# Joining four partition groups of softmax maxima and sums by scalar copies instead of tensor transposes

## The chip, the cores and the metric

The kernel runs on one core of a Trainium2 chip. A core has engines that run side by side, each working through its own instruction queue in order: PE (TensorE) multiplies matrices, with PEld as its weight loads; DVE (VectorE), ACT (ScalarE) and POOL (GpSimd) work on tiles; SP (SyncE) issues most DMAs. SBUF is the on-chip memory with 128 partitions, PSUM the memory that PE writes its results to. The metric is device time in microseconds of one execution.

## The reference

```
xn = layernorm(x)                                   # x: 2048 x 640
q  = xn @ wq                                        # 32 heads of 128
k, v = the last 512 rows of each head's cache
s  = softmax(q k^T / sqrt(128)) v, all heads, @ wo  # 2048 x 640
g  = silu(relu(xn @ w1 + b1)^2 @ w2 + b2)           # 640 -> 1728 -> 640
out = x + s * g
```

All data are float32. The softmax runs over 512 keys, with the row maximum subtracted before the exponential.

## The kernel before

**Products.** Each float32 operand is split into a rounded part (`hi`) and a rest (`lo`), and a product is three matmuls: hi*hi, hi*lo, lo*hi (`triple`). ACT makes hi by a copy, DVE or POOL makes lo by a subtraction.

**Stages.** First comes the gate network for three of the four 512-row tiles, up to about 300 us. Then come the 128 attention units that fill most of the time: `units` runs over two halves of the rows, 16 pairs of heads, two row tiles of a half, and the two heads of a pair. One unit `i` is one head against 512 queries. The gate network of the last row tile is worked in after that, with parts of it in the first three units (`early_up`, `late_relu`, `late_square`, `early_split`).

**One unit.** Scores are held transposed, keys on partitions and queries in columns: 512 keys are 4 chunks of 128 partitions, in two PSUM tiles of two banks each, `s` (`s_mm`). A query's maximum and sum thus lie across partitions. They are found so:

- `max_fold` runs once for each of the two score tiles. It calls `fold`, a DVE reduction over a 128 x 1024 tile that transposes each 32 x 32 block on the way, so that each group of 32 partitions gives its own maximum of every query. The result `rdm` has 4 partition groups x 32 lines, and in its columns the 4 key chunks x 16 query blocks.
- `gather` (DVE) reduces the 4 chunks, giving `r1m` with 128 x 16 elements.
- `turn` (PE) transposes it into PSUM, `ptm`, 16 x 128, and so brings the four partition groups side by side.
- `row` (DVE) reduces the four groups into `rowm`, 16 x 32. Then SP stores these 512 numbers to DRAM (`m_d`) and loads them back, broadcast to all 128 partitions (`bm`).
- `shift` (DVE) subtracts `bm` from the two score tiles, which frees their banks for the next unit's `s_mm`; `expo` (ACT) takes the exponential; `p_hi` (ACT) and `p_lo` (POOL) split it into `pt`; `s_add` (POOL) adds the two halves to `su`.
- The sums go the same way, one period later: `s_fold` on `su` in SBUF (tile `rds`), `gather` (`r1s`), `turn` (`pts`), `row` (`rows`, with a reciprocal), DRAM (`s_d`), broadcast (`bs`).
- `v_mm` multiplies `pt` with the values into `o`; `o_norm` (DVE) scales `o` by `bs`; `o_hi` and `o_lo` split it into `ot`; `r_mm` (PE) and `r_acc` (DVE, tile `acc`) bring it through the output weights.

In between, `q_mm`, `q_hi` and `q_lo` make the queries of unit `i + 2`, and `load_raw` and `prep` load and split the next weights (on ACT the copies `wk`, `wq`, `wv`, `wo`, on POOL their rests).

**Order.** All of this is written into a list `plan` by `at(when, f, ...)` and issued sorted by `when`, in a nominal period of 12.4. The engines that are called through `Ordered` keep that order in their queues, whatever is ready. So an instruction that waits holds up all that is behind it on its engine. The instructions of the units carry line 72, that of the helper, in the profile, and are told apart by their tiles.

Of the kernel before, what the change touches and what calls it, by code (L numbers as in the profile page):

```python
# [8 lines left out]
F32 = mybir.dt.float32  # L9
F32R = mybir.dt.float32r  # L10
AF = mybir.ActivationFunctionType
ALU = mybir.AluOpType
AX = mybir.AxisListType

P = 128
NT = 512
# [4 lines left out]
def kernel(  # L21
# [21 lines left out]
    FC = (F + P - 1) // P  # L43
    KC = W // P
# [8 lines left out]
    dpool = ctx.enter_context(tc.tile_pool(name="dram", bufs=1, space=bass.MemoryType.DRAM))  # L53

    ident = cpool.tile([P, P], F32, name="ident")
# [8 lines left out]
    class Ordered:  # L64
# [13 lines left out]
    pe, dve, act, pool, sp = (  # L78
        Ordered(e) for e in (nc.tensor, nc.vector, nc.scalar, nc.gpsimd, nc.sync)
    )  # L80
# [18 lines left out]
    psx = ctx.enter_context(tc.tile_pool(name="psx", bufs=1, space=PSUM))  # L99

    FA = FC - 3
# [76 lines left out]
    def ln_rows(t, mv, xs):  # L178
        pm = psx.tile([P, NT], F32, tag="x", name=f"pmv{t}")
        nc.tensor.transpose(pm[: 2 * NB, :P], mv.rearrange("p a b -> p (a b)"), ident)  # L180
        row = xp.tile([2 * NB, P], F32, tag="lr", name=f"lr{t}", bufs=1)
        nc.vector.tensor_copy(row, pm[: 2 * NB, :P])
        d = dpool.tile([2, NT], F32, name=f"mv_d{t}")
        nc.sync.dma_start(d.rearrange("a (b p) -> (a b) p", p=P), row)
        bc = []
        for i in range(2):
            m = xp.tile([P, D], F32, tag="mr", name=f"mr{t}_{i}")[:, :NT]
            nc.sync.dma_start(m, d[i : i + 1, :].to_broadcast([P, NT]))
            bc.append(m)
        return bc, xs  # L190
# [136 lines left out]
    def mlp_step(n):  # L327
# [47 lines left out]
    PERIOD = 12.4  # L375
    B32 = 32
    AHEAD = 2
    NQ = NT // B32
# [4 lines left out]
    XT, ACC, KT, VV, WQ, WO, Q, E, SC, MB, RD, PT, PO, OT, RB, QPS, FX, CL, PRS, RAW = (  # L383
        {} for _ in range(20)
    )
# [81 lines left out]

    def fold(rd, k, src, op):
        dve.tensor_reduce(
            rd[:, k * NQ * 2 : (k + 1) * NQ * 2],  # L470
            src.rearrange("p c (b i) -> p (c b) i", i=B32),
            axis=AX.X,
            op=op,
            apply_transpose=True,
        )

    def max_fold(i, k):
        if k == 0:
            RD[i, "m"] = ap.tile([P, KC * NQ], F32, tag="rd", name=f"rdm{i}", bufs=3)
        fold(RD[i, "m"], k, SC[i, k], ALU.max)  # L480

    def gather(i, what):
        rd = RD.pop((i, what))
        n = rd.shape[1] // NQ
        r1 = ap.tile([P, NQ], F32, tag="r1", name=f"r1{what}{i}", bufs=4)
        dve.tensor_reduce(
            r1,
            rd.rearrange("p (c b) -> p b c", b=NQ),
            axis=AX.X,
            op=ALU.max if what == "m" else ALU.add,  # L490
        )
        RD[i, what] = r1

    def turn(i, what):
        pm = psx.tile([P, NT], F32, tag="x", name=f"pt{what}{i}")
        pe.transpose(pm[:NQ, :P], RD.pop((i, what)), ident)
        RD[i, what] = pm

    def row(i, what):
        pm = RD.pop((i, what))  # L500
        r = ap.tile([NQ, B32], F32, tag="row", name=f"row{what}{i}", bufs=4)
        dve.tensor_reduce(
            r,
            pm[:NQ, :P].rearrange("p (a i) -> p i a", i=B32),
            axis=AX.X,
            op=ALU.max if what == "m" else ALU.add,
        )
        if what == "s":
            dve.reciprocal(r, r)
        d = dpool.tile([NQ, B32], F32, tag=f"{what}_d", name=f"{what}_d{i}", bufs=4)  # L510
        sp.dma_start(d, r)
        bc = ap.tile([P, NT], F32, tag=f"b{what}", name=f"b{what}{i}", bufs=2)
        sp.dma_start(bc, d.rearrange("a b -> (a b)")[None, :].to_broadcast([P, NT]))
        (MB if what == "m" else RB)[i] = bc
# [25 lines left out]
        pool.tensor_tensor(RD[i, "su"], E[i, 0], E[i, 1], op=ALU.add)  # L540

    def s_fold(i):
        RD[i, "s"] = ap.tile([P, 2 * NQ], F32, tag="rd", name=f"rds{i}", bufs=3)
        fold(RD[i, "s"], 0, RD.pop((i, "su")), ALU.add)

    def v_mm(i, c):
        hf, g, t, h = units[i]
# [75 lines left out]
    LW, LH, LPH, LPY, LR = {}, {}, {}, {}, {}  # L623
# [98 lines left out]
        else:  # L722
            act.activation(r, ph, AF.Relu, bias=bias)

    def late_square(f):
        pool.tensor_tensor(LR[f], LR[f], LR[f], op=ALU.mult)

    def late_split(f):
        n = chunks[f][1]
# [83 lines left out]
    ap = ctx.enter_context(tc.tile_pool(name="at", bufs=2))  # L813
# [4 lines left out]
    def at(when, f, *a):  # L818
        plan.append((max(when, 0.0), len(plan), f, a))
# [16 lines left out]
    for t in range(TPH):  # L836
        for c in range(DC):
            k, late = divmod(c + 1 - t, 2)
# [17 lines left out]
    for i in range(NU):  # L856
        t0 = i * PERIOD

        def on(when, f, *a):
            at(t0 + when, f, *a)  # L860

        hf, g, t, h = units[i]
        for c in range(KC):
            on(0.68 * c, s_mm, i, c)
        if i + AHEAD < NU:
            q_at = 3.45 if i % G and i > UPG else 4.3
            for c in range(DC):
                on(q_at + 0.68 * c, q_mm, i + AHEAD, (c,))
            on(q_at + 3.5, q_hi, i + AHEAD)
            on(q_at + 4.1, q_lo, i + AHEAD)  # L870
        on(1.4, max_fold, i, 0)
        on(2.8, max_fold, i, 1)
        on(3.95, gather, i, "m")
        on(5.0, turn, i, "m")
        on(5.4, row, i, "m")
        on(10.4, shift, i, 0)
        on(11.6, shift, i, 1)
        on(11.7, expo, i, 0)
        on(12.7, p_hi, i, 0)
        on(13.8, expo, i, 1)  # L880
        on(14.8, p_hi, i, 1)
        on(13.9, p_lo, i, 0)
        on(16.2, s_add, i)
        on(PERIOD + 6.2, s_fold, i)
        on(PERIOD + 7.4, gather, i, "s")
        on(PERIOD + (8.45 if i < FC - FA - 1 else 9.2), turn, i, "s")
        on(PERIOD + 9.6, row, i, "s")
        on(18.6, p_lo, i, 1)
        for c in range(KC):
            on(PERIOD + 8.5 + 0.68 * c, v_mm, i, c)  # L890
        on(2 * PERIOD + 4.2, o_norm, i)
        on(2 * PERIOD + 4.9, o_hi, i)
        on(2 * PERIOD + 5.5, o_lo, i)
        if i % G == G - 1:
            for d in range(DC):
                last = i == NU - G - 1
                if i < NU - 1:
                    for when, js in (R_AT_END if last else R_AT)[d]:
                        on(when, r_mm, i, d, js, (R_BANK_END if last else R_BANK)[d])
                    on(when + 0.68 * len(js), r_acc, i, d)  # L900
                if g == NG - 1 and hf == 0:
                    w = (NU // 2 + 9 + 4 * (t * DC + d)) * PERIOD
                    for k, n in enumerate("sxg"):
                        at(w + k * PERIOD - 0.6, load_finish, n, 0, t, d)
                    at(w + 3 * PERIOD - 0.7, finish, 0, t, d)
# [10 lines left out]
    for item in order:  # L916
        kind, n = item[0], int(item[1:] or 0)
# [37 lines left out]
    for f, u in sorted(UP_AT.items()):  # L955
        at(LOAD.get(f, PREP.get(f - 2, 0) + 0.9), late_load, 1, f)
        when = PREP.setdefault(f, u - 5.0)
        at(when, late_prep, 1, f)
        for c in range(DC):
            at(u + 0.68 * c, late_up, f, UP_BANK[f] if f < len(UP_BANK) else (f + 1) % 2, c)  # L960
        relu, square, split = STEPS_AT.get(f, (u + 3.5, u + 4.3, u + 5.7))
        at(relu, late_relu, f, "kv"[f % 2])
        at(square, late_square, f)
        at(split, late_split, f)
# [8 lines left out]
    for k, f in enumerate(range(FA, FC)):  # L973
        t0 = k * PERIOD
        for c in range(DC):
            at(t0 + 8.0 + 0.1 * c, early_up, f, 0, c)
        at(t0 + 10.6, late_relu, f, "s")
        at(t0 + 12.0, late_square, f)
        at(t0 + PERIOD + 7.6, early_split, f)
    at(z + 2.0, late_x)  # L980
    for d in range(DC):
# [51 lines left out]
```

## Time and profile before

| | us |
|---|---|
| three runs, median (lowest to highest) | 2020.71 (2017.9 to 2021.19) |
| profiled execution, its own time | 2021.47 |
| its span, first to last instruction | 2019.7 |
| PE busy | 1987.9 (98%) |
| DVE busy | 1535.8 (76%) |
| POOL busy | 1375.4 (68%) |
| ACT busy | 985.8 (49%) |

The profile is one execution. Engine lines give busy time, share of the span and number of instructions. The chain of work that ended last is followed back from the last instruction, at each step to what released it; its shares say on what the end depended. A group line names the code line, engine, operation, the tile written and the tiles read, shapes and count, then busy time and the mean ns of one, then the idle time of the engine just before these instructions and what ended it. A wait line says who waited for whom, for how long in all, how many times, and the longest. A timeline line has the start, the time until the last of the merged instructions ended, the engine, and in brackets the idle time before. The granted clock of PE was 0.999 of full speed.

### The profile page before, as it was taken

What the parts mean: (1) busy time and instruction counts of PE and PEld (TensorE: products, weight loads), DVE (VectorE), ACT (ScalarE), POOL (GpSimd) and SP (SyncE); (2) the same over time, 40 slices, a digit from 0 to 9 for tenths busy, and PEclk for the clock granted to TensorE, in tenths of its full rate; (3) what the DMA queues carried; (4) which work ended last, traced back from release to release, by engine and by line L of the source; (5) the groups of instructions that cost most, each with busy time, mean ns of one, the idle gap of its engine ahead of it and who ended that gap; (6) DMA issues with size and microseconds to landing.
All of it is one profiled execution on the core that took longest, in us unless ns stands there. A gap on an engine that the chain in (4) does not pass through costs nothing.

```text
span 2019.7 us, 25025 instructions
## 1 busy us (share of the span) xinstructions
PE 1987.9 (98%) x8832; PEld 1609.3 (80%) x8832; DVE 1535.8 (76%) x2252; ACT 985.8 (49%) x1266; POOL 1375.4 (68%) x754
## 2 busy tenths in 40 slices
PE   7999999999999999999999999999999999999998
PEld 6788887788888888888887788787878888788877
DVE  5532337788888888888887778888888888888864
ACT  4432335555555555555554455555555555555533
POOL 1121227788777777777777788788888888877841
PEclk9999999999999999999999999999999999999999
DMA  4431454322333332333335433333333333333344
GB/s 140 128 113 29 177 196 132 99 90 89 90 89 89 90 89 90 90 91 90 91 96 159 154 95 105 110 110 111 110 110 111 110 112 110 96 91 90 106 146 140
DMA packets 126862, 220.32 MB, mean 109 GB/s; under 512 B 21542, under 2 KB 36304, under 8 KB 125456
## 3 DMA queue, kind: packets, MB, share of 16 engines
q1 hardware_dynamic: 123744, 204.28, 33.6%
q0 software_dynamic: 2992, 14.43, 1.8%
q8 instruction: 70, 1.15, 0.2%
q14 instruction: 56, 0.46, 0.1%
HBM read 194.26 MB, written 24.39 MB: 108 GB/s over the span
## 4 chain that ended last, share of the span: by engine, by line
PE 88%; DMA 6%; DVE 2%; POOL 1%; ACT 1%; issue 1%; SPq 0%; POOLq 0%; DVEq 0%
PE pq L72 20%; PE r L72 19%; PE s L72 17%; PE o L72 15%; DMA bm<-m_d 2%; PE py L96 2%; PE py L97 2%; PE py L95 2%; PE ph L96 2%; PE ph L95 2%; PE ph L97 2%; PE ly L72 2%; DMA m_d<-rowm 1%; PE lu L72 1%; DMA w1r<-in_w_dram 1%; DVE e L72 1%
## 5 line engine op out<-in xcount | busy, mean ns | idle before, releaser
L72 POOL TENSOR_TENSOR pt<-e,pt 128x1024 fp32r<-128x1024 f32 x256 | 617.5, 2412 | 296.1 <-ACT pt L72 296.1
L72 PE MATMUL r<-ot,wo 128*128 128x512 f32 x1920 | 496.9, 389 | 0.5 <-DVE acc L72 0.5
L72 PE MATMUL pq<-ax,wq 128*128 128x512 f32 x1920 | 473.1, 396 | 0.1
L72 ACT ACTIVATE e<-e 128x1024 f32<-128x1024 f32 x256 | 269.5, 1053 | 370.6 <-DVE e L72 331.6
L72 PEld LDWEIGHTS r<-ot,wo 128*128 128x128 f32 x1920 | 360.2, 188 | 75.9 <-DVE acc L72 0.9
L72 PEld LDWEIGHTS pq<-ax,wq 128*128 128x128 f32 x1920 | 350.9, 188 | 84.5 <-DMA ax<-xT_d 0.9
L72 PE MATMUL o<-pt,wv 128*128 128x512 f32 x1536 | 386.5, 398 | 0.4 <-POOL pt L72 0.3
L72 PE MATMUL s<-q,wk 128*128 128x512 f32 x1536 | 372.2, 391 | 9.1 <-DVE e L72 9.0
L72 DVE TRANSPOSE_TENSOR_REDUCE rdm<-s 128x32 f32<-128x1024 f32 x256 | 319.3, 1249 | 60.6 <-PE s L72 46.3
L72 PEld LDWEIGHTS s<-q,wk 128*128 128x128 f32 x1536 | 286.4, 188 | 76.9 <-DVE e L72 16.3
L72 PEld LDWEIGHTS o<-pt,wv 128*128 128x128 f32 x1536 | 278.7, 188 | 70.8 <-POOL pt L72 1.5
L72 DVE TENSOR_TENSOR e<-s,bm 128x1024 f32<-128x1024 f32 x256 | 299.9, 1212 | 37.5 <-DMA bm<-m_d 33.7
L72 POOL TENSOR_TENSOR su<-e,e 128x1024 f32<-128x1024 f32 x128 | 308.5, 2410 | 0.0
L72 ACT ACTIVATE pt<-e 128x1024 fp32r<-128x1024 f32 x256 | 271.7, 1061 | 7.8
L72 DVE TENSOR_TENSOR acc<-r,acc 128x512 f32<-128x512 f32 x300 | 202.5, 675 | 2.8 <-PE r L72 2.8
L237 POOL TENSOR_TENSOR r<-r 128x512 f32<-128x512 f32 (+1 forms) x42 | 44.1, 1049 | 227.5 <-ACT r L278 207.9
L72 ACT ACTIVATE ot<-o 128x512 fp32r<-128x512 f32 x128 | 76.8, 600 | 228.3 <-DVE o L72 228.3
L72 DVE TRANSPOSE_TENSOR_REDUCE rds<-su 128x32 f32<-128x1024 f32 x128 | 158.5, 1239 | 10.7 <-POOL su L72 9.0
L72 ACT ACTIVATE q<-pq 128x512 fp32r<-128x512 f32 x128 | 76.7, 599 | 164.8 <-PE pq L72 164.7
L72 DVE TENSOR_TENSOR ot<-o,ot 128x512 fp32r<-128x512 f32 x128 | 88.5, 691 | 32.0 <-ACT ot L72 32.0
L239 DVE TENSOR_TENSOR h<-r,h 128x512 fp32r<-128x512 f32 (+1 forms) x42 | 29.0, 690 | 107.7 <-ACT h L238 107.6
L72 POOL TENSOR_TENSOR wq<-qr,wq 128x640 fp32r<-128x640 f32 x62 | 98.5, 1588 | 4.0 <-ACT wq L72 2.8
(122 smaller groups left out, 2152.6 us busy)
## 6 DMA issues: line engine op xcount, KB each, us to landing
bm<-m_d SPq DMA_DIRECT2D x128, 256.0 KB, 3.3
bs<-s_d SPq DMA_DIRECT2D x128, 256.0 KB, 4.0
qr<-in_wq_dram SPq DMA_DIRECT2D x64, 320.0 KB, 4.4
or<-in_wo_dram SPq DMA_DIRECT2D x64, 320.0 KB, 4.5
kr<-in_kT_dram SPq DMA_DIRECT2D x64, 256.0 KB, 4.4
vr<-in_v_dram SPq DMA_DIRECT2D x64, 256.0 KB, 4.3
xT_d<-xT POOLq DMA_DIRECT2D x6, 1280.0 KB, 7.5
xb<-in_x_dram SPq DMA_DIRECT2D x16, 320.0 KB, 3.5
```

Source lines behind the costliest of these rows:

```text
L72: ins = method(*args, **kwargs)
L95: nc.tensor.matmul(ps, ah, bh, start=first and i == 0, stop=False)
L96: nc.tensor.matmul(ps, ah, bl, start=False, stop=False)
L97: nc.tensor.matmul(ps, al, bh, start=False, stop=last and i == n - 1)
L237: nc.gpsimd.tensor_tensor(r, r, r, op=ALU.mult)
L239: nc.vector.tensor_tensor(lo, r, raw(hi), op=ALU.subtract)
```

## The change

- `fold` reads its source with another order of columns: before, a block of 32 is 32 adjacent queries (`(b i)`); after, it is every 16th query (`(i b)`). The reads within a block are then 16 elements, 64 bytes, apart.
- The fold's tile grows to `[128, 4, n]` (`fold_tile`). The fold writes slot 0 of it.
- `gather` no longer reduces. It is now three ACT copies that bring partition groups 1 to 3 into slots 1 to 3 of partitions 0 to 31, of 32 x 64 elements for the maxima and 32 x 32 for the sums.
- `turn`, the PE transpose, is gone, for maxima and sums, as are the tiles `r1` and `ptm`, `pts`.
- `row` is one DVE reduction over chunks and groups together: 32 partitions, 16 results of 16 elements each for the maxima and of 8 for the sums. It writes 32 x 16 instead of 16 x 32, and so do the reciprocal and the store to DRAM. The order of the 512 numbers in DRAM is the same.
- In the plan, `row` of the maxima moves from 5.4 to 4.45, `gather` of the sums from 7.4 to 8.0, `row` of the sums from 9.6 to 8.5.
- Three squares of the last row tile's gate network, in the first three units, move from POOL to DVE.

```
 
     def fold(rd, k, src, op):
         dve.tensor_reduce(
-            rd[:, k * NQ * 2 : (k + 1) * NQ * 2],
-            src.rearrange("p c (b i) -> p (c b) i", i=B32),
+            rd[:, k * NQ * 2 : (k + 1) * NQ * 2].rearrange("p (c b) -> p c b", b=NQ),
+            src.rearrange("p c (i b) -> p c b i", i=B32),
             axis=AX.X,
             op=op,
             apply_transpose=True,
         )
 
+    def fold_tile(what, i):
+        n = (KC if what == "m" else 2) * NQ
+        return ap.tile([P, P // B32, n], F32, tag=f"rd{what}", name=f"rd{what}{i}", bufs=2)
+
     def max_fold(i, k):
         if k == 0:
-            RD[i, "m"] = ap.tile([P, KC * NQ], F32, tag="rd", name=f"rdm{i}", bufs=3)
-        fold(RD[i, "m"], k, SC[i, k], ALU.max)
+            RD[i, "m"] = fold_tile("m", i)
+        fold(RD[i, "m"][:, 0, :], k, SC[i, k], ALU.max)
 
     def gather(i, what):
-        rd = RD.pop((i, what))
-        n = rd.shape[1] // NQ
-        r1 = ap.tile([P, NQ], F32, tag="r1", name=f"r1{what}{i}", bufs=4)
-        dve.tensor_reduce(
-            r1,
-            rd.rearrange("p (c b) -> p b c", b=NQ),
-            axis=AX.X,
-            op=ALU.max if what == "m" else ALU.add,
-        )
-        RD[i, what] = r1
-
-    def turn(i, what):
-        pm = psx.tile([P, NT], F32, tag="x", name=f"pt{what}{i}")
-        pe.transpose(pm[:NQ, :P], RD.pop((i, what)), ident)
-        RD[i, what] = pm
+        rd = RD[i, what]
+        for a in range(1, P // B32):
+            act.activation(rd[:B32, a, :], rd[a * B32 : (a + 1) * B32, 0, :], AF.Copy)
 
     def row(i, what):
-        pm = RD.pop((i, what))
-        r = ap.tile([NQ, B32], F32, tag="row", name=f"row{what}{i}", bufs=4)
-        dve.tensor_reduce(
-            r,
-            pm[:NQ, :P].rearrange("p (a i) -> p i a", i=B32),
-            axis=AX.X,
-            op=ALU.max if what == "m" else ALU.add,
-        )
+        rd = RD.pop((i, what))[:B32].rearrange("p a (c b) -> p b (a c)", b=NQ)
+        r = ap.tile([B32, B32], F32, tag="row", name=f"row{what}{i}", bufs=4)[:, :NQ]
+        dve.tensor_reduce(r, rd, axis=AX.X, op=ALU.max if what == "m" else ALU.add)
         if what == "s":
             dve.reciprocal(r, r)
-        d = dpool.tile([NQ, B32], F32, tag=f"{what}_d", name=f"{what}_d{i}", bufs=4)
+        d = dpool.tile([B32, NQ], F32, tag=f"{what}_d", name=f"{what}_d{i}", bufs=4)
         sp.dma_start(d, r)
         bc = ap.tile([P, NT], F32, tag=f"b{what}", name=f"b{what}{i}", bufs=2)
         sp.dma_start(bc, d.rearrange("a b -> (a b)")[None, :].to_broadcast([P, NT]))
...
         pool.tensor_tensor(RD[i, "su"], E[i, 0], E[i, 1], op=ALU.add)
 
     def s_fold(i):
-        RD[i, "s"] = ap.tile([P, 2 * NQ], F32, tag="rd", name=f"rds{i}", bufs=3)
-        fold(RD[i, "s"], 0, RD.pop((i, "su")), ALU.add)
+        RD[i, "s"] = fold_tile("s", i)
+        fold(RD[i, "s"][:, 0, :], 0, RD.pop((i, "su")), ALU.add)
 
     def v_mm(i, c):
         hf, g, t, h = units[i]
...
         else:
             act.activation(r, ph, AF.Relu, bias=bias)
 
-    def late_square(f):
-        pool.tensor_tensor(LR[f], LR[f], LR[f], op=ALU.mult)
+    def late_square(f, eng=pool):
+        eng.tensor_tensor(LR[f], LR[f], LR[f], op=ALU.mult)
 
     def late_split(f):
         n = chunks[f][1]
...
         on(1.4, max_fold, i, 0)
         on(2.8, max_fold, i, 1)
         on(3.95, gather, i, "m")
-        on(5.0, turn, i, "m")
-        on(5.4, row, i, "m")
+        on(4.45, row, i, "m")
         on(10.4, shift, i, 0)
         on(11.6, shift, i, 1)
         on(11.7, expo, i, 0)
...
         on(13.9, p_lo, i, 0)
         on(16.2, s_add, i)
         on(PERIOD + 6.2, s_fold, i)
-        on(PERIOD + 7.4, gather, i, "s")
-        on(PERIOD + (8.45 if i < FC - FA - 1 else 9.2), turn, i, "s")
-        on(PERIOD + 9.6, row, i, "s")
+        on(PERIOD + 8.0, gather, i, "s")
+        on(PERIOD + 8.5, row, i, "s")
         on(18.6, p_lo, i, 1)
         for c in range(KC):
             on(PERIOD + 8.5 + 0.68 * c, v_mm, i, c)
...
         for c in range(DC):
             at(t0 + 8.0 + 0.1 * c, early_up, f, 0, c)
         at(t0 + 10.6, late_relu, f, "s")
-        at(t0 + 12.0, late_square, f)
+        at(t0 + 12.0, late_square, f, dve)
         at(t0 + PERIOD + 7.6, early_split, f)
     at(z + 2.0, late_x)
     for d in range(DC):
```

## The prediction

> **What bounds the kernel now.** I read the page first, then the PE timeline of one steady unit, then the other engines of the same unit, then the waits. The profiled execution took 2021.47 us, 1.8 us more than its span, and stands 0.76 us above the median of the three runs (2020.71). About 0.2% (4 us) is what a measurement of this kernel can tell from no change.
>
> ```profile
> span 2019.7 us, 25025 instructions
> PE 1987.9 (98%) x8832; PEld 1609.3 (80%) x8832; DVE 1535.8 (76%) x2252; ACT 985.8 (49%) x1266; POOL 1375.4 (68%) x754
> PE 88%; DMA 6%; DVE 2%; POOL 1%; ACT 1%; issue 1%; SPq 0%; POOLq 0%; DVEq 0%
> ```
>
> PE carries 88% of the chain that ended last. It runs an order written by hand, so what leaves its queue shortens the path unless another loop then ends last. One unit on PE, from its first score matmul to the next unit's:
>
> ```profile
> 945.36 2.88 PE L72 MATMUL s<-q,wk 128*128 128x512 f32 x12
> 948.08 0.84 PE L72 MATMUL r<-ot,wo 128*128 128x512 f32 x3
> 948.76 2.20 PE L72 MATMUL pq<-ax,wq 128*128 128x512 f32 x9
> 950.80 0.27 PE L72 MATMUL ptm<-ident,r1m 128*16 128x128 f32 x1
> 950.83 1.62 PE L72 MATMUL pq<-ax,wq 128*128 128x512 f32 x6
> 952.29 1.52 PE L72 MATMUL r<-ot,wo 128*128 128x512 f32 x6
> 953.65 1.52 PE L72 MATMUL o<-pt,wv 128*128 128x512 f32 x6
> 955.01 0.27 PE L72 MATMUL pts<-ident,r1s 128*16 128x128 f32 x1
> 955.04 1.62 PE L72 MATMUL o<-pt,wv 128*128 128x512 f32 x6
> 956.50 1.52 PE L72 MATMUL r<-ot,wo 128*128 128x512 f32 x6
> 957.86 2.88 PE L72 MATMUL s<-q,wk 128*128 128x512 f32 x12
> ```
>
> The unit is 12.50 us with no gap on PE. Starts, not durations, give the price of an instruction here, since matmuls overlap. Twelve score matmuls take 948.08 - 945.36 = 2.72 us, 0.227 each. The 15 query matmuls with the transpose ptm among them take 952.29 - 948.76 = 3.53, against 15 x 0.227 = 3.40; the 12 output matmuls with pts take 956.50 - 953.65 = 2.85, against 2.72. So each transpose costs PE **0.13 us**, not the 0.27 its record shows.
>
> The second bound is a loop through the maximum. The score banks of a unit are free for the next one's scores only when shift has read them, and shift waits for the maximum, which goes through DRAM. The same unit on DVE, SP, ACT and POOL:
>
> ```profile
> 946.92 2.61 DVE L72 TRANSPOSE_TENSOR_REDUCE rdm<-s 128x32 f32<-128x1024 f32 x2 [0.45 <-PE s L72]
> 949.46 0.65 DVE L72 TENSOR_TENSOR acc<-r,acc 128x512 f32<-128x512 f32 x1
> 950.03 0.25 DVE L72 TENSOR_REDUCE r1m<-rdm 128x16 f32<-128x64 f32 x1
> 950.20 0.69 DVE L72 TENSOR_TENSOR o<-o,bs 128x512 f32<-128x512 f32 x1
> 951.11 0.28 DVE L72 TENSOR_REDUCE rowm<-ptm 16x32 f32<-16x128 f32 x1 [0.22 <-PE ptm L72]
> 952.16 1.24 DVE L72 TRANSPOSE_TENSOR_REDUCE rds<-su 128x32 f32<-128x1024 f32 x1
> 953.43 0.19 DVE L72 TENSOR_REDUCE r1s<-rds 128x16 f32<-128x32 f32 x1
> 953.54 0.68 DVE L72 SCALAR_TENSOR_TENSOR q<-pq,q 128x512 fp32r<-128x512 f32 x1
> 954.14 0.69 DVE L72 TENSOR_TENSOR acc<-r,acc 128x512 f32<-128x512 f32 x1
> 955.32 0.28 DVE L72 TENSOR_REDUCE rows<-pts 16x32 f32<-16x128 f32 x1 [0.50 <-PE pts L72]
> 956.09 2.36 DVE L72 TENSOR_TENSOR e<-s,bm 128x1024 f32<-128x1024 f32 x2
> 951.42 0.32 SPq L72 DMA_DIRECT2D m_d<-rowm  x1
> 952.76 0.33 SPq L72 DMA_DIRECT2D bm<-m_d  x1
> 950.92 0.60 ACT L72 ACTIVATE ot<-o 128x512 fp32r<-128x512 f32 x1 [1.88 <-DVE o L72]
> 952.98 0.62 ACT L72 ACTIVATE wk<-kr 128x512 fp32r<-128x512 f32 x1
> 953.51 0.73 ACT L72 ACTIVATE wo<-or 128x640 fp32r<-128x640 f32 x1
> 959.71 2.40 POOL L72 TENSOR_TENSOR pt<-e,pt 128x1024 fp32r<-128x1024 f32 x1 [2.65 <-ACT pt L72]
> ```
>
> Folds until 949.53, rowm until 951.39, its store at 951.42, the broadcast load at 952.76, shift at 956.09. The first of the two shifts ends half of 2.36 later, at 957.27, and PE wants that bank at 957.86: **0.59 us of slack**. Some units have none:
>
> ```profile
> PEld s L72 <- DVE e L72: 16.3, 23, 2.2
> ```
>
> In 23 units (I take one wait for one unit) PE stood still for shift. So I count about 105 of the 128 units as bound by PE and 23 as bound by the loop.
>
> **PE, removed.** 2 x 0.13 = 0.26 us per unit. In 105 units that is 27.3 us. The period could fall to 12.24 if the loop allows it: with the slack above, 0.59 - 0.26 = 0.33 us is left.
>
> **The small operations.** What DVE loses and gains needs the price of a short reduction and of a read with a gap of 64 bytes between elements:
>
> ```profile
> L72 DVE TENSOR_REDUCE r1m<-rdm 128x16 f32<-128x64 f32 x128 | 33.0, 258 | 2.4
> L72 DVE TENSOR_REDUCE r1s<-rds 128x16 f32<-128x32 f32 x128 | 24.1, 188 | 4.4
> L72 DVE TENSOR_SCALAR sc<-mv 128x4 f32<-128x4 f32 x4 | 0.7, 170 | 0.1
> L72 DVE RECIPROCAL rows<-rows 16x32 f32<-16x32 f32 x128 | 43.7, 341 | 4.4
> L72 DVE RECIPROCAL sc<-sc 128x4 f32<-128x4 f32 x4 | 0.7, 177 | 2.4 <-ACT sc L154 2.4
> L182 DVE COPY lr<-pmv 8x128 f32<-8x128 f32 x3 | 0.8, 277 | 6.2 <-PE pmv L180 6.2
> L154 ACT ACTIVATE sc<-sc 128x4 f32<-128x4 f32 x4 | 0.8, 206 | 2.0 <-DVE sc L72 1.9
> ```
>
> In PSUM the trace has the answer: rowm reads 128 elements 128 bytes apart in 0.28 us, and the copy lr reads 128 adjacent ones in 277 ns. A stride costs DVE nothing there, so I leave the two maximum folds at 2.61 us the pair. They decide more than anything else, and the slower rival below is this step failing.
>
> In SBUF the only strided reads are r1m and r1s, 64 bytes apart like the new fold of the sums. An adjacent element costs about 1.04 ns: the fold rds at 1.24 us less a fixed 170, over 1024. From r1s to r1m, 32 more elements cost 70 ns, 2.19 each. But against the fixed part, 170 ns for 4 elements, so about 166, r1s lies below 166 + 33 and r1m gives (258 - 166)/64 = 1.44. The price lies between 1.04 and 2.19; I take **1.44**, since r1m is the longest strided read. Then the fold of the sums goes from 1.24 to 1.65 us (2.42 at the top end), the new rowm with 256 elements takes 166 + 256 x 1.44 = 535 ns (432 to 680), and rows with 128 takes 350 (300 to 400). The reciprocal has 16 columns instead of 32: between 177 ns with 4 and 341 with 32 lies about 250.
>
> [...]
>
> A scalar copy: 206 ns with 4 columns, 0.62 us with 512 (wk), so 0.82 ns a column: 255 ns with 64, 229 with 32. Two ACT operations overlap by 0.09 (wk starts at 952.98 with 0.62, wo at 953.51). Three copies take 0.255 + 2 x 0.165 = 0.58 us for the maxima and 0.51 for the sums. In 128 units ACT gets 140 us more, from 49% to about 56% of the span.
>
> **The maximum's path.** The copies wait for the second fold, at 949.53. ACT is free then: it stood idle for 1.88 us before 950.92. They end at about 950.15. Queued behind them is the copy of ot, which waits for the DVE step o in any case. Meanwhile DVE does acc, then o, 0.17 earlier without r1m, until 950.72, so the copies hide behind DVE. rowm then runs to 951.26 instead of 951.39, with no wait on ptm: **0.13 us earlier** (0.23 earlier to nothing). Without the cover of acc and o, the copies would put 0.6 us on the loop. The store of rowm writes 32 pieces of 64 bytes instead of 16 of 128; from its issue to that of the load that waits for it are 1.34 us (951.42 to 952.76). The new one moves the same bytes, so I bound the change by 0 and, as an estimate, a tenth of this, 0.13 us, and take 0. In the 23 loop-bound units the gain is then 0.13 each, 3.0 us.
>
> **The sums' path.** DVE no longer waits 0.50 us for pts. The fold ends at 953.81 at my price, the query step and acc end at about 955.1, rows at 955.45 and the reciprocal at 955.7, before shift at 956.09: nothing is lost. The three copies sit on ACT ahead of wk and wo and push wk from 952.98 to about 954.35 (953.84 + 0.51), 1.4 us; POOL, which takes both, has 2.65 us of idle time before its next pt, so this is covered, and would cost up to 1.4 us a unit on the pt chain if that idle time were gone. On SP's queue the store and load of the sums move from 9.6 to 8.5 in the plan, ahead of a few loads of ax; I count nothing, with 5 us either way. The three early squares move from POOL to DVE; at 0.69 us each on DVE, like the step o, they cost 0 to 2 us, and I take 0, as they come behind shift with no fold ready.
>
> **Sum.** 27.3 + 3.0 = 30.3 us less: 2021.5 - 30.3 = 1991.2, and 1990.4 against the median. I say **1991 us**. With all units gaining 0.26 it would be 1988; early loads of the sums could take it to 1984.
>
> **Rivals.** *SBUF strides cost 2.19 ns.* The fold of the sums ends at 954.58, the query step, acc, rows and the reciprocal at about 956.5; shift starts 0.4 late and its first half ends at 957.7, while PE wants it at 957.60. That is 0.1 us in each unit with this second acc, 64 units or 6 us; the loop-bound units gain nothing (3 us) and the slack that absorbs late loads is gone, some 3 to 12 us more. Result 2003, from 1996 to 2012. For it speaks the step from r1s to r1m; against it that the fixed part would have to be 118 ns, below any SBUF row.
>
> *Slower: the strided folds of PSUM become the loop.* At the same 1.15 ns more per element, each fold takes 1.18 us more, both lie in the loop, and the first shift ends 2.36 - 0.13 = 2.2 us later, at 959.5 instead of PE's 957.60. The period becomes 14.1, 1.6 more than now, times 128: 2230 us. It decides from about 0.23 us a fold, a fifth of its time, where the remaining slack of 0.33 + 0.13 is spent; from 0.36 a fold the whole gain is gone. Against it stands the pair rowm and lr; for it, that neither of these is a transposing reduction.
>
> *No gain.* The row leaves late because ACT or a semaphore holds the copies until 0.7 us after o (the slack of 0.33 + 0.13, and 0.26 for what PE gave), and the loop takes back what PE gave: 2017 to 2025. ACT's idle time speaks against it.
>
> **How the numbers follow.** Forecast 0.52 (1984 to 1996), SBUF strides 0.29 (1996 to 2012), PSUM folds 0.13, no gain 0.06 (mostly within 0.2%). The range 1984 to 2012 leaves out 0.19. The first two make faster 0.81; no gain makes same 0.05; the PSUM case and the rest of no gain make slower 0.14.
>
> **What would show it.** In the profile after: no ptm and pts on PE, a steady unit of about 12.24 us, rdm still near 1250 ns, rds near 1650, rowm near 535, copies on ACT near 250, PE's wait for shift no longer than now. A fold rdm above 1.5 us, or PE waiting for shift in most units, proves the prediction wrong.

## The result and the profile after

| | before | after |
|---|---|---|
| median (lowest to highest), us | 2019.87 (2017.9 to 2021.19, 4 runs) | 1991.7 (1989.57 to 1993.97, 4 runs) |
| ratio after / before | | 0.9861, 95% interval 0.9849 to 0.9872 |
| profiled execution, us | 2021.47 | 1989.57 |

The change makes the kernel 28 us faster. The prediction was 1991. The spans of the two profiled executions differ by 31.9 us. The page of after, the same three lines as before:

```profile
span 1987.8 us, 25109 instructions
PE 1956.7 (98%) x8576; PEld 1606.2 (81%) x8576; DVE 1597.2 (80%) x1999; ACT 1184.1 (60%) x2034; POOL 1374.5 (69%) x751
PE 83%; DMA 6%; DVE 6%; POOL 3%; ACT 2%; issue 1%; SPq 0%; DVEq 0%; ACTq 0%; POOLq 0%
```

PE has 256 matmuls fewer and is busy 31.2 us less, the size of the gain. DVE and ACT are both busier, and PE is still 98% busy: the work moved from the engine that bounds the kernel to two that do not. One steady unit in the PE timeline of after:

```profile
946.48 2.88 PE L72 MATMUL s<-q,wk 128*128 128x512 f32 x12
949.20 1.52 PE L72 MATMUL r<-ot,wo 128*128 128x512 f32 x6
950.56 3.56 PE L72 MATMUL pq<-ax,wq 128*128 128x512 f32 x15
953.96 0.84 PE L72 MATMUL r<-ot,wo 128*128 128x512 f32 x3
954.64 2.88 PE L72 MATMUL o<-pt,wv 128*128 128x512 f32 x12
957.36 1.52 PE L72 MATMUL r<-ot,wo 128*128 128x512 f32 x6
958.72 1.59 PE L72 MATMUL s<-q,wk 128*128 128x512 f32 x6
```

From score matmul to score matmul are 12.24 us, against 12.50. The 15 query matmuls now take 953.96 - 950.56 = 3.40 instead of 3.53, the 12 output matmuls 2.72 instead of 2.85. The other engines in the same unit:

```profile
948.04 2.61 DVE L72 TRANSPOSE_TENSOR_REDUCE rdm<-s 128x32 f32<-128x1024 f32 x2 [0.32 <-PE s L72]
950.68 0.79 ACT L72 ACTIVATE rdm<-rdm 32x64 f32<-32x64 f32 x3 [0.40 <-DVE rdm L72]
950.76 0.69 DVE L72 TENSOR_TENSOR acc<-r,acc 128x512 f32<-128x512 f32 x1
951.37 0.69 DVE L72 TENSOR_TENSOR o<-o,bs 128x512 f32<-128x512 f32 x1
951.97 0.58 DVE L72 TENSOR_REDUCE rowm<-rdm 32x16 f32<-32x256 f32 x1
952.58 0.33 SPq L72 DMA_DIRECT2D m_d<-rowm  x1
953.93 0.33 SPq L72 DMA_DIRECT2D bm<-m_d  x1
955.32 0.71 ACT L72 ACTIVATE rds<-rds 32x32 f32<-32x32 f32 x3 [0.56 <-DVE rds L72]
956.06 0.37 DVE L72 TENSOR_REDUCE rows<-rds 32x16 f32<-32x128 f32 x1 [0.19 <-ACT rds L72]
957.31 2.36 DVE L72 TENSOR_TENSOR e<-s,bm 128x1024 f32<-128x1024 f32 x2 [0.61 <-DMA bm<-m_d]
```

The copies for the maxima run from 950.68 to 951.47, and DVE is at acc and o until rowm starts at 951.97, so rowm waits for nothing. The first shift ends at 957.31 + 1.18 = 958.49, when the unit's last r matmuls still run, and scores start at 958.72. The groups, and two rows of the waits:

```profile
L72 DVE TRANSPOSE_TENSOR_REDUCE rdm<-s 128x32 f32<-128x1024 f32 x256 | 318.8, 1248 | 51.5 <-PE s L72 35.1
L72 DVE TRANSPOSE_TENSOR_REDUCE rds<-su 128x32 f32<-128x1024 f32 x128 | 252.2, 1970 | 17.2 <-POOL su L72 16.1
L72 ACT ACTIVATE rdm<-rdm 32x64 f32<-32x64 f32 x384 | 98.2, 256 | 52.4 <-DVE rdm L72 48.9
L72 DVE TENSOR_REDUCE rowm<-rdm 32x16 f32<-32x256 f32 x128 | 74.1, 579 | 5.7 <-ACT rdm L72 5.7
L72 DVE TENSOR_REDUCE rows<-rds 32x16 f32<-32x128 f32 x128 | 46.1, 360 | 13.6 <-ACT rds L72 13.5
L72 DVE RECIPROCAL rows<-rows 32x16 f32<-32x16 f32 x128 | 30.9, 241 | 4.4
```

```profile
PE s L72 <- DVE e L72: 6.4, 9, 2.4
DVE e L72 <- DMA bm<-m_d: 38.0, 60, 3.0
```

The folds of the maxima in PSUM cost the same with the stride (1248 ns, before 1249), the fold of the sums in SBUF 1970 instead of 1239. PE waits for shift 9 times. The same row of before:

```profile
PE s L72 <- DVE e L72: 9.0, 13, 1.8
```

So PE itself waited 13 times in before; the 23 waits that the prediction shows are those of its weight loads.

Where the time went can be read by stretch, from the starts of the units' first score matmuls. The second line of each pair is the excess over the period of an undisturbed steady unit, the shortest one (12.493 before, 12.240 after), that is, what was lost to waits. A few of the first eight periods are shorter than that, and the excess is net of them:

| us | units 0 to 8 | 8 to 59 | 59 to 67 | 67 to 127 | rest of the span |
|---|---|---|---|---|---|
| before | 100.0 | 639.1 | 109.1 | 753.3 | 418.3 |
| of it excess | 0.0 | 1.9 | 9.2 | 3.7 | |
| after | 99.7 | 626.1 | 103.0 | 739.7 | 419.3 |
| of it excess | 1.8 | 1.8 | 5.1 | 5.3 | |

The undisturbed periods differ by 0.253 us, times 127 that is 32.1 us of gain, and the waits add up to nearly the same in both kernels, 15 and 14 us.

### The profile page after: what moved, and what is told of

It is laid out like the page before. It is cut to its first block, busy times and chain, and to the rows that moved or that the text cites. A ratio compares the mean times of both kernels' runs of the same rounds, so it can differ in the third digit from the quotient of the medians.

```text
span 1987.8 us, 25109 instructions
## 1 busy us (share of the span) xinstructions
PE 1956.7 (98%) x8576; PEld 1606.2 (81%) x8576; DVE 1597.2 (80%) x1999; ACT 1184.1 (60%) x2034; POOL 1374.5 (69%) x751
## 4 chain that ended last, share of the span: by engine, by line
PE 83%; DMA 6%; DVE 6%; POOL 3%; ACT 2%; issue 1%; SPq 0%; DVEq 0%; ACTq 0%; POOLq 0%
PE r L72 19%; PE pq L72 18%; PE s L72 16%; PE o L72 15%; DMA bm<-m_d 2%; PE ly L72 2%; PE py L96 2%; PE py L97 2%; PE py L95 2%; PE ph L96 2%; PE ph L97 2%; PE ph L95 2%; DMA w1r<-in_w_dram 1%; PE lu L72 1%; POOL pt L72 1%; DMA m_d<-rowm 1%
## 5 line engine op out<-in xcount | busy, mean ns | idle before, releaser
L72 PE MATMUL pq<-ax,wq 128*128 128x512 f32 x1920 | 456.5, 389 | 0.9 <-DMA ax<-xT_d 0.9
L72 PEld LDWEIGHTS pq<-ax,wq 128*128 128x128 f32 x1920 | 360.3, 188 | 76.3 <-DMA ax<-xT_d 1.7
L72 PE MATMUL o<-pt,wv 128*128 128x512 f32 x1536 | 372.1, 390 | 1.7 <-POOL pt L72 1.1
L72 DVE TRANSPOSE_TENSOR_REDUCE rdm<-s 128x32 f32<-128x1024 f32 x256 | 318.8, 1248 | 51.5 <-PE s L72 35.1
L72 PEld LDWEIGHTS o<-pt,wv 128*128 128x128 f32 x1536 | 287.2, 188 | 65.8 <-POOL pt L72 6.5
L72 DVE TRANSPOSE_TENSOR_REDUCE rds<-su 128x32 f32<-128x1024 f32 x128 | 252.2, 1970 | 17.2 <-POOL su L72 16.1
L72 ACT ACTIVATE rds<-rds 32x32 f32<-32x32 f32 x384 | 87.6, 228 | 128.6 <-DVE rds L72 125.6
L72 POOL TENSOR_TENSOR wv<-vr,wv 128x512 fp32r<-128x512 f32 x64 | 83.1, 1298 | 78.1 <-ACT wv L72 78.1
L72 ACT ACTIVATE rdm<-rdm 32x64 f32<-32x64 f32 x384 | 98.2, 256 | 52.4 <-DVE rdm L72 48.9
```

The source lines that it names most:

```text
L72: ins = method(*args, **kwargs)
```

## The experiments

The kernel before itself took 2013 to 2021 us, depending on the chip, so each ratio is to its runs on the same chip. Every edit is made to the kernel after.

**Transposes back on PE, for nothing.** They transpose a slice of the identity into a tile that nobody reads; the copies stay.

```
+    def turn(i, what):
+        pm = psx.tile([P, NT], F32, tag="x", name=f"pt{what}{i}")
+        pe.transpose(pm[:NQ, :P], ident[:, :NQ], ident)
...
+        on(5.0, turn, i, "m")
+        on(PERIOD + (8.45 if i < FC - FA - 1 else 9.2), turn, i, "s")
```

> The kernel after, with two PE transposes per unit put back at their old places in the order. They read the constant identity (16 columns) and nothing reads what they write, so PE does the old work and nobody waits for it. Theory (the time came from PE's queue, 0.13 us per transpose): about 33 us slower than the kernel after, 2020 to 2027, units of about 12.50 us. Rival (the time came from shorter waits on the paths of the maxima and sums, and PE had time to spare): within 5 us of the kernel after, 1987 to 1997.

Measured: 2014.97, ratio 0.9974 (0.9964 to 0.9985). PE's line of the page:

```profile
PE 1982.8 (99%) x8832; PEld 1610.2 (80%) x8832; DVE 1599.2 (80%) x1999; ACT 1184.4 (59%) x2034; POOL 1375.3 (68%) x751
```

The steady unit is 12.49 us again, exactly that of before, and 23 of the 28 us are gone. So PE's queue is the cause of most of the gain. The number expected was missed by 5 us: the units' excess is 6.3 us here, less than either kernel's, and the late stores below, of which this kernel has few, go with that. In the profiled executions that excess is 8.5 us less than in before, and in the medians 5 us remain; what of the change they come from was not tested.

**The folds read adjacent columns again.** The copies and the row stay, over other columns, so this kernel leaves out that each query gets its own maximum and sum.

```
-            src.rearrange("p c (i b) -> p c b i", i=B32),
+            src.rearrange("p c (b i) -> p c b i", i=B32),
```

> The kernel after, with all folds reading adjacent columns as before; the rest is that of after, so the maxima and sums come out under other queries' places. Theory (the stride costs DVE only in SBUF, and there it is covered by DVE's idle time before shift): the fold of the sums goes from 1.97 to 1.24 us, that of the maxima stays at 1.25, the time within 4 us of the kernel after. Rival (the dearer fold of the sums lies on the path): 0.3 us or more a unit comes back in the units with two later acc steps, 10 to 40 us faster than after.

Measured: 1985.6, ratio 0.9828 (0.9815 to 0.9842), against after's 0.9861.

```profile
L72 DVE TRANSPOSE_TENSOR_REDUCE rds<-su 128x32 f32<-128x1024 f32 x128 | 158.9, 1242 | 15.4 <-POOL su L72 13.9
```

```profile
DVE e L72 <- DMA bm<-m_d: 112.4, 126, 2.9
```

The fold of the sums is back at 1242 ns, 0.73 us less a unit, 93 us of DVE time. By the ratios the kernel gains 0.33%, 6 to 7 us; the spans differ by 3.0. The expectation was within 4 us, which the ratios miss by 2 to 3. The steady unit stays at 12.24. What the stride uses up is DVE's idle time: shift waits for the row of the maxima in 126 units here, in 60 in after, and in 54 others of after DVE works right up to shift. The stride lies nearly, but not wholly, off the path.

**One half at a time.** The first kernel joins the maxima the new way and the sums the old way; the second does the reverse. Shown is the plan of the first.

```
-        on(PERIOD + 8.0, gather, i, "s")
-        on(PERIOD + 8.5, row, i, "s")
+        on(PERIOD + 7.4, old_gather, i, "s")
+        on(PERIOD + (8.45 if i < FC - FA - 1 else 9.2), turn, i, "s")
+        on(PERIOD + 9.6, old_row, i, "s")
```

> Only the maxima go the new way (strided fold, copies on ACT, one DVE reduction); the sums keep adjacent columns, the DVE gather, the PE transpose and their old times. Theory (PE's queue): half of the gain, 14 to 18 us faster than before, 2002 to 2007, units of about 12.37 us. Rival (the loop through the maximum was what bound the units): nearly all of the gain, 1990 to 1996.

> Only the sums go the new way; the maxima keep adjacent columns, the DVE gather, the PE transpose and their old times. Theory (PE's queue): the other half, 14 to 18 us faster than before, 2002 to 2007. Rival (the loop through the maximum): nearly no gain, 2015 to 2021.

Measured: the maxima alone 2000.54, ratio 0.9902 (0.9889 to 0.9916), 20 us; the sums alone 2016.17, ratio 0.9979 (0.997 to 0.9988), 4 us. Each shortens the undisturbed steady unit to 12.37, by one transpose, worth 16 us. So the price of a transpose holds in both, and the rest is mostly waits: the excess over that period is 9.2 us with the maxima alone and 22.0 with the sums alone, against 14.8 in before. For the sums this gives 9 us, as the spans of the profiled executions do (2019.7 and 2010.7); the median lies 3.6 above the profiled execution, and no trace shows why. The large excess goes with stores of the maxima that are slow. One of them, in the timeline of the kernel with the sums alone:

```profile
949.80 0.28 DVE L72 TENSOR_REDUCE rowm<-ptm 16x32 f32<-16x128 f32 x1 [0.22 <-PE ptm L72]
950.11 0.33 SPq L72 DMA_DIRECT2D m_d<-rowm  x1
952.50 0.33 SPq L72 DMA_DIRECT2D bm<-m_d  x1
955.80 2.36 DVE L72 TENSOR_TENSOR e<-s,bm 128x1024 f32<-128x1024 f32 x2 [1.28 <-DMA bm<-m_d]
957.17 1.17 PE L72 MATMUL s<-q,wk 128*128 128x512 f32 x4 [0.59 <-DVE e L72]
```

Between the issue of the store and of the load are 2.39 us, where 1.34 is usual; shift waits 1.28 us and PE stands still for 0.59. Such stores (over 1.5 us) come in 30 of 106 steady units here (8 to 58 and 67 to 121), in 17 of before, in 5 of after, in 4 of the kernel with the transposes for nothing and in 7 of that with the maxima alone. The last section says what they coincide with.

**After again**, as the base for the next three.

> The kernel after unchanged, on this chip, for the comparison with the other three of this call: 1987 to 1996.

Measured: 1985.65, ratio 0.9863 (0.9848 to 0.9878).

**The squares back on POOL.** The second unit takes 14.08 us in after and 13.15 in before; the three squares on DVE fall in the first three units.

```
-        at(t0 + 12.0, late_square, f, dve)
+        at(t0 + 12.0, late_square, f)
```

> The kernel after, with the three early squares back on POOL. Theory (they lie outside what bounds the units): within 3 us of the kernel after. Rival (one of them on DVE is what made the second unit 14.08 us long instead of 13.15): 1 to 3 us faster than after.

Measured: 1986.01, ratio 0.9868 (0.9853 to 0.9882), no difference. The second unit stays at 13.97, so the squares aren't its cause. In the kernel below with only the rows at their old places it takes 12.34; what makes it long stays open.

**Each copy made twice.**

```
-        for a in range(1, P // B32):
+        for a in (1, 2, 3, 1, 2, 3):
```

> The kernel after, with each of the three ACT copies made twice, so ACT gets about 185 us more and each join 0.7 to 0.8 us. Theory (the copies are covered by the DVE steps acc and o, but by little, and the row of the maxima then starts 0.3 to 0.5 us later): the slack of about 0.5 us before the next scores is nearly used up, 4 to 25 us slower than after. Rival (ACT's load has cover enough): within 3 us of after. Rival (the copies are on the path already): 0.8 us a unit, about 100 us slower.

Measured: 2041.47, ratio 1.0139 (1.0122 to 1.0156), 56 us more than after on the same chip. From the timeline and the waits:

```profile
946.93 1.65 ACT L72 ACTIVATE rdm<-rdm 32x64 f32<-32x64 f32 x6 [0.16 <-DVE rdm L72]
948.61 0.59 DVE L72 TENSOR_REDUCE rowm<-rdm 32x16 f32<-32x256 f32 x1 [0.31 <-ACT rdm L72]
951.71 1.49 ACT L72 ACTIVATE rds<-rds 32x32 f32<-32x32 f32 x6 [0.70 <-DVE rds L72]
953.23 0.36 DVE L72 TENSOR_REDUCE rows<-rds 32x16 f32<-32x128 f32 x1 [0.98 <-ACT rds L72]
```

```profile
DVE rows L72 <- ACT rds L72: 88.1, 127, 1.6
DVE rowm L72 <- ACT rdm L72: 68.9, 128, 1.8
```

The copies of the maxima end 0.3 us after o in this unit, and rowm waits in every unit, where after had 12 such waits. The row of the sums waits too, 0.98 us here, with shift behind it on DVE. The steady unit is 12.53 us in the median, and now shift sets it: scores start 0.15 us after the first shift ends, in each of the 106 steady units. So the cover that the prediction named has an end: 0.86 us more of copies for the maxima and 0.78 for the sums together make the kernel slower than before. What each of them would do alone is not shown. In the 64 steady units for which the trace has its landing, the row of the maxima lands 0.02 to 0.25 us before shift starts, and DVE works right up to shift in nearly all, so both paths come due at about the same time. The prediction had the row of the sums done well before shift; here its waits are the larger ones.

**acc behind the row of the maxima.** If the loop through the maximum still cost something, taking acc out from between the fold and rowm should help.

```
-                    on(when + 0.68 * len(js), r_acc, i, d)
+                    done = when + 0.68 * len(js)
+                    on(done + {1: 0.5, 2: 1.2}.get(d, 0.0), r_acc, i, d)
```

> The kernel after, with the DVE step acc that stands between the fold and the row of the maxima moved behind that row in the order (two of the five steps of each pair of heads). Theory (what is left of stalls is the loop through the maximum, about 14 us over 127 units at 12.24): the row ends 0.2 to 0.4 us earlier, the stalls are halved, 4 to 9 us faster than after. Rival (the stalls are late DMA and do not depend on DVE's order): within 3 us of after.

Measured: 1983.4, ratio 0.9855 (0.984 to 0.9869).

```profile
DVE rowm L72 <- ACT rdm L72: 35.0, 127, 0.9
DVE e L72 <- DMA bm<-m_d: 15.8, 29, 2.8
```

rowm ends 0.2 to 0.45 us earlier, although it now waits for the copies, and shift waits for the row 29 times instead of 63. The steady unit is 12.24 as before it. The 2 us less come from excess (7.1 us instead of 10.3), but the two intervals overlap: the lowest median measured, and not separable from after.

**The old places in the plan.** The three moved steps at their old times.

```
-        on(4.45, row, i, "m")
+        on(5.4, row, i, "m")
-        on(PERIOD + 8.0, gather, i, "s")
-        on(PERIOD + 8.5, row, i, "s")
+        on(PERIOD + 7.4, gather, i, "s")
+        on(PERIOD + 9.6, row, i, "s")
```

> The kernel after with the old places in the order: the row of the maxima at 5.4, the copies of the sums at 7.4, the row of the sums at 9.6. Theory (of the moves only that of the sums' row counts, since it lets their store and load go out on SP's queue ahead of the loads of ax): the 8 units in which ax is loaded lose 3 to 5 us, the rest 0 to 3, so 3 to 8 us slower than after. Rival (the moves are worth nothing): within 3 us of after.

Measured: 2023.09, ratio 1.0043 (1.003 to 1.0057), slower than before; 3 to 8 us were expected and 36 came. So some place in the plan is worth more than the transposes. Two kernels parted the three moves: in the first only the copies of the sums go back to 7.4, in the second only the two rows go back.

> The kernel after with one of the three old places alone: the ACT copies of the sums at 7.4 instead of 8.0, ahead of q_hi in every second unit, where q_hi is due at 7.8. Theory (ACT waits there for the fold of the sums, which the stride has made 0.73 us longer, and q_hi, q_lo, the row of the sums and shift queue behind it): nearly all of what the three old places cost together, 28 to 42 us slower than after. Rival (it was the rows that moved): within 5 us of after.

> The kernel after with the other two old places: the row of the maxima at 5.4 and that of the sums at 9.6, the copies of the sums at 8.0 as in after. Theory (DVE has no other step between the old and the new places): 0 to 6 us slower than after, the most of it in the 8 units in which ax is loaded, since those loads then go ahead of the sums' store and load. Rival (the rows' places are what counts): 28 to 42 us slower.

Measured: the copies alone 2022.04, ratio 1.0034 (1.0024 to 1.0044); the rows alone 1989.59, ratio 0.9872 (0.9858 to 0.9886). It is all in the copies of the sums. From the timeline and the waits with the copies at 7.4:

```profile
966.66 1.95 DVE L72 TRANSPOSE_TENSOR_REDUCE rds<-su 128x32 f32<-128x1024 f32 x1
968.64 0.71 ACT L72 ACTIVATE rds<-rds 32x32 f32<-32x32 f32 x3 [2.62 <-DVE rds L72]
969.25 0.57 ACT L72 ACTIVATE q<-pq 128x512 fp32r<-128x512 f32 x1
969.86 0.69 DVE L72 SCALAR_TENSOR_TENSOR q<-pq,q 128x512 fp32r<-128x512 f32 x1 [1.25 <-ACT q L72]
971.03 2.28 DVE L72 TENSOR_TENSOR e<-s,bm 128x1024 f32<-128x1024 f32 x2
972.33 2.97 PE L72 MATMUL s<-q,wk 128*128 128x512 f32 x12
```

```profile
DVE q L72 <- ACT q L72: 81.4, 64, 2.2
```

ACT stands 2.62 us at the first copy until the fold of the sums is done, with the copy of q queued behind, whose input is there. DVE then waits 1.25 us for that copy, shift starts late, and scores start 0.16 us after its first half (971.03 + 1.14). This happens in every second unit: 64 waits, against 4 in after, and units of 12.5, with 12.34 between them. Against 12.24 that is some 25 us of the 34 to 35 that the copies alone cost.

**The gap between elements, one size at a time.** One kernel in which four units in turn read with gaps of 1, 2, 4 and 8 elements of 4 bytes.

```
-            src.rearrange("p c (i b) -> p c b i", i=B32),
+            src.rearrange("p c (g i b) -> p c g b i", i=B32, b=st),
...
+        fold(RD[i, "s"][:, 0, :], 0, RD.pop((i, "su")), ALU.add, (1, 2, 4, 8)[i // 4 % 4])
```

> The kernel after, with the gap between the elements that a fold reads at 1, 2, 4 or 8 elements (4 to 32 bytes) instead of 16, a different one in each run of four units; the maxima and sums come out under other queries' places. Theory 1 (in SBUF a price is due wherever the next element lies 16 bytes or more away): the fold of the sums takes 1.24 us at 1 and 2, about 1.97 at 4 and 8; the fold of the maxima, in PSUM, 1.25 at all. Theory 2 (the price grows with the gap): 1.24, 1.3 to 1.4, 1.5 to 1.6, 1.7 to 1.8. The time lies within 6 us of the kernel after, mostly faster.

Measured in one run, beside 2014.08 of before: 1987.18. The fold of the sums with gaps of 1, 2, 4 and 8 elements:

```profile
755.40 1.24 DVE L72 TRANSPOSE_TENSOR_REDUCE rds<-su 128x32 f32<-128x1024 f32 x1
804.36 1.24 DVE L72 TRANSPOSE_TENSOR_REDUCE rds<-su 128x32 f32<-128x1024 f32 x1
816.48 2.01 DVE L72 TRANSPOSE_TENSOR_REDUCE rds<-su 128x32 f32<-128x1024 f32 x1
865.67 2.16 DVE L72 TRANSPOSE_TENSOR_REDUCE rds<-su 128x32 f32<-128x1024 f32 x1 [0.23 <-POOL su L72]
```

Nearly all of the price, 0.77 of 0.92 us, comes in one step at 4 elements, 16 bytes. The folds of the maxima in PSUM take 1.25 us at every gap, 1248 ns in the mean of 256. What makes the step in SBUF, and why the reads in PSUM have none, is not shown.

## Why the prediction was right, and where it was not

- **Transposes on PE, 0.13 us each.** Right: the unit went from 12.50 to 12.24, and came back to 12.49 when the transposes did.
- **105 units of 0.26 and 23 of 0.13.** The sum, 30.3, came out (31.9 between the spans, 28 between the medians), the split did not. All units got shorter by 0.25, 32.1 us in all. The 23 waits were those of weight loads; PE itself waited 13 times. They marked units in which something came late once, not units with a lower gain: the excess over the undisturbed period was 14.8 us and is 14.0. That period's change times the units would have been the better sum. That 1991 was met to 1 us is in part luck: the units gained 2 us more than was summed, and the medians moved 4 us less than the spans.
- **PSUM folds unchanged.** Right to 1 ns (1248 against 1249), and the same 1248 in the mean at gaps of 4 to 32 bytes. The slower rival rested on this step alone and fell with it.
- **SBUF stride, 1.44 ns an element.** Mis-sized: with the fixed 170 ns the fold gives (1970 - 170)/1024 = 1.76, inside the bounds of 1.04 and 2.19. rowm took 579 ns (535 foreseen), rows 360 (350), the reciprocal 241 (250). The rival of 2003 us didn't come: in 60 units the reciprocal still ends before the row of the maxima arrives, on which shift waits. In 54 others DVE works right up to shift, and undoing the stride moved the time by 3 to 7 us, so the cover isn't whole, where the sum had nothing for it.
- **Copies on ACT, 0.58 and 0.51 us.** Too short. They take 0.79 and 0.71, three full durations, without the 0.09 of overlap that was read off two copies of 512 and 640 columns. ACT went to 60% instead of 56%. For the maxima it cost nothing because acc and o still cover it, with 0.5 us to spare (951.47 against 951.97). For the sums the row waited 13.5 us in all, 65 times, ahead of shift on DVE; what that cost was not measured.
- **rowm 0.13 us earlier.** Relative to the unit's first score matmul it ended at 6.03 before, and ends at 6.07 and 5.85 now, in units of either kind: 0.04 later to 0.18 earlier, against bounds of 0 to 0.23.
- **The store at no change.** Right in the usual case, 953.93 - 952.58 = 1.35 us against 1.34. The cases that aren't usual, 17 late stores before and 5 now, weren't seen at all.
- **Sums, SP queue, squares at nothing.** With the rows at their old times, and so their DMAs at their old place in SP's queue, the ratio is 0.9872, with the squares on POOL 0.9868, in after itself 0.9861 and 0.9863: nothing that shows.
- **What was left out.** The prediction weighed the copies of the sums against wk and wo behind them. It didn't say what their place relative to the copy of q is worth: 34 to 35 us, more than the whole gain, had they alone stayed at 7.4. It took the plan's 8.0 as given, and here that was enough.

## What to carry to other kernels

Where one engine with an order written by hand is 98% busy, price what leaves its queue by the distance of starts, take the change of the undisturbed period times the units for the gain, and count waits separately. Work given to a less busy engine was free here only as long as the rows beside it covered it (0.79 us of copies for the maxima were covered; 1.65, with 1.49 for the sums, made the kernel 56 us slower): read the cover in microseconds (here 0.5), and look at what is queued behind the new instruction on its engine, since one step earlier in ACT's order cost 34 to 35 us, more than the 28 that the change brought. A stride had its price by memory here: none in PSUM (1.25 us at gaps of 4 to 64 bytes), 0.7 to 0.9 us on a fold of 1024 elements in SBUF from 16 bytes on (1.24 us below that).

## What the runs showed of the hardware

- **A slow small store.** The store of the maxima, 2 KB, normally takes 1.34 us from its issue to that of the load that waits for it, in before and in after. Late ones, up to 2.41 us in before, mostly coincide with packets of another queue:

```profile
q8 instruction: 70, 1.15, 0.2%
```

This row of the DMA queues of before says 70 packets with 1.15 MB, 16 KB each; a packet is under way for about 0.96 us, and over the units they come 28.3 us apart on average, some 2.25 units, or every 256 of PE's matmuls and weight loads. Over the steady units of all fourteen kernels profiled, 78 of 119 late stores had such a packet under way 0.43 us after their issue, and none of 1365 stores in time (in before 15 of 17 and none of 89, in after 3 of 5 and none of 101). That moment is picked from the data; at the issue itself it is 62 and 23. This is a coincidence that holds one way; no run here moved the packets alone, so that they cause the delay is not shown, and some 40 late stores go with something else. In the kernel with the sums alone each of the 30 has a packet under way at some time between store and load; why they meet so often there is not known.

- **A step at 16 bytes.** DVE's transposing reduction of 128 x 1024 in SBUF: 1.24 us with gaps of 4 and 8 bytes, 2.01 at 16, 2.16 at 32, in the kernel with the gaps, and 1.97 at 64 in after. The cost is not monotonic.
- **Small copies within one tile did not overlap on ACT.** Three of 256 ns take 0.79 us in after, six 1.65 with each copy made twice.
